# Output stores on SyncE's queue and a new order of the steps in a gated-linear-attention and hard-swish kernel

## Chip, cores and metric

The kernel runs on one core of a Trainium2 chip. The metric is the device time of one execution in microseconds; three executions of the kernel before took 554.13, 555.63 and 557.94 us. The profile shown is of one further execution, whose span is 554.3 us and which took 556.35 us by the timing. The clock granted to TensorE was 0.999 of full speed throughout.

## What is computed

A recurrent attention with decay over 4 batches, 8 heads, 768 tokens and head dimension 48, whose result is fed as 3072 tokens of 384 features to a two-layer block with a hard-swish gate. Cut to what matters:

```python
for t in range(S):
    state = alpha[:, :, t, :, None] * state + np.einsum('bhd,bhe->bhde', k[:, :, t], v[:, :, t])
    y[:, :, t] = np.einsum('bhd,bhde->bhe', q[:, :, t], state)
...
x = np.ascontiguousarray(attn_out.transpose(0, 2, 1, 3)).reshape(B * S, H * D)
h = x @ w_in                      # 384 -> 2048
relu6 = np.clip(h + 3.0, 0.0, 6.0)
g = h * relu6 / 6.0
return (g @ w_out).astype(np.float32)   # 2048 -> 384
```

All is in float32.

## The kernel before

**Chunks and groups.** The 3072 tokens are cut into 24 chunks of 128 (six to a batch), and two chunks make one of 12 groups of 256 tokens. The attention goes chunk by chunk. The two-layer block goes group by group. The first group and the preparation of the weights are the opening; this text says "behind the opening" for what comes from the step P.1.0 on.

**The attention of one chunk j.** Loads bring alpha, k and q (`la`, `lk`, `lq`: four DMAs each from chunk 6 on, line 284) and v (`lv`: eight DMAs from chunk 8 on, line 299). VectorE (DVE) transposes them in blocks of 32 (`tk`, `tq`, `ca`, line 318), runs two scans over alpha (`r` line 341, `p` line 352) and scales k and q with them (`k`, `q`, line 364). TensorE (PE) forms the scores (`sc`, lines 383 and 385), DVE masks them (`m`, line 391), and PE multiplies them with v (`yi`, lines 529 and 533; `yx` adds the part of the earlier state, line 549). For the state, k is turned by DVE (`kt`), written to DRAM and read back in another layout (`kw` line 459, one DMA; `kr` line 466, four DMAs), PE multiplies it with v (`u`, line 488), DVE adds (`sm`, line 509), GpSimd (POOL) applies the decay (`st`, line 471). `vh` (line 399) copies half of v on ScalarE (ACT), and `cy` (line 557) copies the chunk's output out of PSUM.

The products of `sc`, `yi`, `yx` and `u` use parts of the 128 x 128 array (tiles of 48 x 64, 128 x 32 and less). They are many and short: 32 matmuls for a `sc` or a `u`, 64 for a `yi`, 24 for a `yx`. This text calls them small-tile products, and a stretch of such steps on PE with no full-array product between them a run.

**The two-layer block of one group g.** The first layer is done with 20 products instead of 24 block products (`M.g.i.bank`, line 693; four column blocks and two matmul records each, eight records to a step), on sums of the inputs (`xc`) and of the weights (`y`). ACT copies some products to SBUF (`n`, line 699), DVE joins them (`o`, lines 630 to 634), ACT and DVE apply the gate (`e` line 587, `h` line 591). The second layer has seven products instead of eight (`P.g.i`, line 796, sixteen records to a step) on sums of the gated values (`s`, lines 740 and 757). `K` (line 775, ACT) saves parts, `G` (line 812 on DVE, and 809 on ACT for G.g.3) adds them up into one of four buffers `oh`, and `O` (`store2`, line 817) stores that quarter of the group's output. Stores of the opening's group are `so` (`store`, line 620).

**What sets the order.** The program is a list of words, each a step with its numbers, written out by hand under a manual schedule. Each step issues its instructions to its engines in the order of the list; every engine goes through its own instructions strictly in that order, and waits where a tile isn't ready or a buffer not yet free. A last number in a word chooses a buffer: one of four PSUM banks for full products (`M`, `P`), one of four for the small ones (`sc`, `u`, `yi`), a slot in SBUF or an `oh` buffer. Loads go through SyncE's queue (SP). In the kernel before, the stores go through ACT's queue, in between ACT's copies and gates.

```python
    def store2(g, i):
        row, col = PLACES[i]
        j = G * g + row
        nc.scalar.dma_start(out=out[j * C : (j + 1) * C, col * HD : (col + 1) * HD],
                            in_=oh_t.pop((g, i)))
```

Of the kernel before, what the change touches and what calls it, by code (L numbers as in the profile page):

```python
# [8 lines left out]
FP = mybir.dt.float32  # L9
# [8 lines left out]
def kernel(  # L18
# [32 lines left out]
    nc = tc.nc  # L51
    B, H, S, D = q.shape
    NTOK, DM = out.shape
    C = 128
# [6 lines left out]
    G = 2  # L61
# [7 lines left out]
    consts = ctx.enter_context(tc.tile_pool(name="consts", bufs=1))  # L69
# [15 lines left out]
    v0 = consts.tile([C, H, 64], FP, tag="vfirst")  # L85
# [42 lines left out]
    st, sm = [], []  # L128
# [490 lines left out]
    def store(c):  # L619
        nc.scalar.dma_start(out=out[c * C : (c + 1) * C, :], in_=os_t.pop(c))  # L620
# [193 lines left out]
    def store2(g, i):  # L814
        row, col = PLACES[i]
        j = G * g + row
        nc.scalar.dma_start(out=out[j * C : (j + 1) * C, col * HD : (col + 1) * HD],
                            in_=oh_t.pop((g, i)))
# [22 lines left out]
    with tc.manual_schedule():  # L841
# [20 lines left out]
               so.1 b.0.2 lv.7.0 y.4 y.13 ca.6 yx.5 y.0 b.0.3 cy.5 r.6 la.8 bo.0 cy.4 x.1 y.3 lv.8.1  # L862
               P.1.0.3 s.1.0.0 s.1.1.1 P.1.3.0 xc.2.1 x.2 K.1.0 s.1.2.3 xc.2.3 tk.7 s.1.3.2 P.1.2
               K.1.1 y.10 y.8 P.1.1.2 y.9 y.16 xc.2.4 s.1.4 P.1.4 x.3 K.1.2 y.15 s.1.5 xc.2.5 P.1.5
               G.1.1.0 P.1.6 G.1.3.1 y.17 y.19 G.1.0.2 y.18 y.12 y.20 M.2.0.1 tq.7 G.1.2.3 M.2.15.2
               M.2.16 lv.6.2 n.2.0.8 xc.2.6 y.21 y.23 M.2.1 xc.2.0 lk.6 lq.8 tk.6 xc.2.7 M.2.7.0 k.6
               xc.2.8 ca.7 xc.2.9 xc.2.2 r.7 vh.8 n.2.1.9 M.2.2 O.1.2 n.2.7.10 o.2.4.0 p.6 ca.8 lq.9
               la.10 la.9 lk.8 lk.9 xc.2.10 kb.6.0 M.2.8 O.1.1 n.2.2.11 M.2.3 M.2.4 n.2.4.12 o.2.0.0
               k.7 y.14 q.6 e.2.0.0 h.2.0 M.2.18.3 M.2.17 M.2.5 n.2.5.13 ck.6 M.2.9 o.2.1.0 e.2.1.1
               kb.7.3 sc.6.2.1 M.2.10 ck.7 u.6.0 u.7.3 n.2.10.14 M.2.11 n.2.11.15 p.7 m.6 q.7  # L870
               sc.7.1.2 M.2.12 n.2.18.12 M.2.19 y.22 M.2.6.1 h.2.1 n.2.12.11 M.2.13 sm.6 r.8 y.24
               o.2.3.0 m.7 tq.8 yi.6.0 yi.7.1 n.2.13.11 cy.6 st.7 yx.7 o.2.7.0 o.2.2.0 o.2.5.0 cy.7
               xc.3.0 xc.3.1 o.2.2.1 e.2.2.0 xc.3.3 o.2.7.1 M.2.14 xc.3.4 xc.3.5 o.2.3.1 P.2.0.3
               M.3.0.2 xc.3.10 xc.3.6 xc.3.7 M.3.7.1 n.3.0.11 M.3.1 o.2.6.0 h.2.2 o.2.6.1 e.2.3.1
               h.2.3 e.2.4.0 h.2.4 tk.8 xc.3.2 e.2.5.1 e.2.7.0 h.2.7 xc.3.8 n.3.1.12 n.3.7.9 K.2.0
               P.2.1.0 h.2.5 G.2.0.3 e.2.6.0 h.2.6 M.3.2 n.3.2.13 s.2.1.10 s.2.0.14 sm.7 s.2.3.15
               M.3.8 k.8 M.3.3 M.3.4 n.3.4.8 P.2.3.0 o.3.0.0 xc.3.9 p.8 s.2.2.10 M.3.9 o.3.1.0
               e.3.1.1 M.3.5 P.2.2 M.3.10 tq.9 kt.8 kw.8 lq.10 lv.9.2 n.3.5.14 K.2.2 s.2.5 P.2.5
               s.2.4 q.8 ca.9 r.9 e.3.0.0 h.3.0 p.9 O.1.0 n.3.10.10 M.3.11 K.2.1 G.2.2.0 P.2.4 tk.9
               q.9 k.9 h.3.1 n.3.11.15 M.3.12 ca.10 n.3.12.8 o.3.3.0 M.3.6.2 M.3.18.0 n.3.18.13  # L880
               sc.8.2.0 sc.9.1.3 M.3.13 M.3.19 n.3.13.8 kr.8 la.12 kt.9 kw.9 m.8 m.9 st.8 u.8.0 sm.8
               st.9 o.3.3.1 o.3.5.0 yi.8.2 yx.8 vh.9 yi.9.1 e.3.5.0 o.3.2.0 tq.10 o.3.6.0 o.3.2.1
               G.2.1.2 cy.8 yx.9 cy.9 M.3.15.0 o.3.7.0 M.3.16 M.3.14 P.2.6 o.3.4.0 M.3.17 xc.4.1
               xc.4.0 xc.4.3 e.3.3.1 o.3.6.1 h.3.3 e.3.2.1 O.2.2 O.2.1 G.2.3.0 xc.4.4 xc.4.5 xc.4.6
               xc.4.7 M.4.0.2 P.3.0.1 M.4.7.3 h.3.2 o.3.7.1 xc.4.8 h.3.5 n.4.0.8 M.4.1 e.3.6.1
               P.3.1.0 lk.10 lv.11.1 lk.11 lq.11 tk.10 e.3.7.0 h.3.7 O.2.0 e.3.4.0 n.4.7.13 xc.4.10
               r.10 p.10 k.10 s.3.1.10 h.3.4 q.10 h.3.6 tq.11 K.3.0 G.3.0.2 n.4.1.14 M.4.2 kr.9
               u.9.3 lv.10.0 s.3.0.12 kt.10 sm.9 xc.4.2 s.3.3.11 xc.4.9 s.3.2.15 st.10 sc.10.0.2
               m.10 n.4.2.9 M.4.3 M.4.4 P.3.3.0 K.3.2 M.4.8 n.4.4.10 P.3.2 K.3.1 O.3.0 so.0 s.3.4
               o.4.0.0 s.3.5 la.11 ca.11 r.11 M.4.9 o.4.1.0 e.4.1.0 tk.11 ca.12 k.11 M.4.5 P.3.5  # L890
               M.4.10 n.4.10.12 e.4.0.1 kw.10 lv.12.2 lk.12 kr.10 lk.13 lq.12 la.13 p.11 q.11
               G.3.2.3 r.12 h.4.1 P.3.4 G.3.1.2 M.4.11 M.4.18.0 vh.10 yi.10.1 tk.12 p.12 yx.10
               u.10.3 sc.11.0.2 k.12 kt.12 lq.13 lv.14.0 kw.12 tq.12 h.4.0 m.11 O.3.1 n.4.11.11
               M.4.12 n.4.12.15 P.3.6 G.3.3.2 M.4.13 n.4.5.9 n.4.18.10 O.1.3 q.12 sm.10 o.4.3.0
               o.4.7.0 M.4.6.1 o.4.3.1 n.4.13.15 vh.11 o.4.2.0 o.4.2.1 e.4.3.0 M.4.15.2 M.4.16
               M.4.19 cy.10 yi.11.0 st.11 yx.11 sc.12.2.3 o.4.4.0 h.4.3 e.4.2.1 h.4.2 O.2.3 cy.11
               xc.5.1 o.4.5.0 o.4.6.0 M.4.14 xc.5.3 xc.5.4 xc.5.5 xc.5.0 o.4.6.1 e.4.6.0 vh.12
               P.4.0.1 K.4.0 M.5.0.0 M.4.17 xc.5.7 tk.13 M.5.7.3 xc.5.6 h.4.6 m.12 e.4.5.1 n.5.0.15
               M.5.1 n.5.1.9 o.4.7.1 ca.13 h.4.5 r.13 e.4.7.0 n.5.7.14 h.4.7 e.4.4.1 O.3.2 P.4.1.2
               h.4.4 s.4.0.10 G.4.0.1 M.5.2 la.14 kr.12 u.12.1 yi.12.0 n.5.2.8 M.5.3 M.5.4 n.5.4.12  # L900
               ca.14 xc.5.8 p.13 M.5.8 s.4.1.11 P.4.3.2 o.5.0.0 xc.5.2 M.5.9 k.13 s.4.2.13 kt.13
               xc.5.10 s.4.3.10 P.4.2 K.4.1 K.4.2 e.5.0.0 O.4.0 tq.13 o.5.1.0 M.5.10 xc.5.9 M.5.5
               s.4.5 P.4.5 q.13 n.5.10.11 M.5.11 r.14 lq.14 lv.13.1 e.5.1.1 cy.12 n.5.11.10 n.5.5.13
               lk.14 tk.14 s.4.4 h.5.0 p.14 sm.12 tq.14 P.4.4 h.5.1 q.14 k.14 st.13 vh.13 M.5.12
               n.5.12.12 M.5.6.0 sc.13.2.3 m.13 sc.14.0.1 o.5.3.0 M.5.13 G.4.1.0 o.5.3.1 G.4.2.3
               n.5.13.8 o.5.2.0 o.5.2.1 yi.13.2 yx.13 cy.13 xc.6.1 xc.6.3 kw.13 lk.15 kr.13 la.15
               u.13.3 M.5.18.2 M.5.14 P.4.6 lv.15.2 la.16 sm.13 st.14 lq.16 ca.15 n.5.18.12 o.5.6.0
               xc.6.4 o.5.6.1 e.5.6.0 xc.6.5 kt.14 xc.6.0 xc.6.6 o.5.7.0 G.4.3.1 M.5.19 M.6.0.0
               xc.6.7 h.5.6 xc.6.8 o.5.5.0 tk.15 M.5.15.3 M.5.16 xc.6.2 lq.15 tq.15 o.5.4.0 n.6.0.8
               vh.14 M.6.1 e.5.2.1 n.6.1.12 P.5.0.1 h.5.2 m.14 r.15 k.15 e.5.3.0 M.6.2 e.5.4.1 h.5.4  # L910
               O.3.3 M.6.7.2 M.5.17 o.5.7.1 p.15 h.5.3 n.6.2.15 M.6.3 n.6.7.9 M.6.8 q.15 e.5.5.1
               h.5.5 K.5.0 M.6.4 n.6.4.14 O.4.3 o.6.0.0 e.5.7.0 kw.14 ca.16 P.5.1.3 M.6.9 M.6.5
               sc.15.2.3 yi.14.0 yx.14 kr.14 u.14.1 s.5.0.13 kt.15 G.5.0.2 h.5.7 o.6.1.0 e.6.1.1
               s.5.1.11 s.5.2.10 P.5.3.3 sm.14 xc.6.10 M.6.10 lk.16 lv.17.1 xc.6.9 tk.16 s.5.4
               s.5.3.13 P.5.2 s.5.5 O.5.0 n.6.10.11 M.6.11 K.5.2 O.4.2 h.6.1 r.16 n.6.5.15 e.6.0.0
               kw.15 kr.15 lk.17 la.18 k.16 p.16 m.15 M.6.18.0 n.6.18.10 o.6.6.0 tk.17 tq.16 h.6.0
               n.6.11.13 o.6.7.0 q.16 K.5.1 P.5.5 kt.16 G.5.2.1 M.6.12 P.5.4 n.6.12.14 M.6.19
               o.6.5.0 o.6.3.0 M.6.13 n.6.13.10 st.15 la.17 ca.17 M.6.6.3 o.6.2.0 r.17 sc.16.1.2
               vh.15 yi.15.3 cy.14 yx.15 lq.17 lv.16.0 kw.16 u.15.0 lk.18 lv.19.2 lk.19 sm.15 st.16
               o.6.3.1 G.5.1.2 cy.15 xc.7.1 xc.7.3 M.6.15.0 M.6.14 xc.7.4 o.6.6.1 M.6.16 o.6.4.0  # L920
               e.6.4.1 e.6.3.0 o.6.2.1 xc.7.5 xc.7.6 P.5.6 M.6.17 xc.7.10 h.6.4 M.7.0.2 e.6.2.1
               n.7.0.14 h.6.2 h.6.3 xc.7.0 xc.7.8 m.16 e.6.6.1 xc.7.9 o.6.7.1 xc.7.7 e.6.5.0 G.5.3.3
               O.5.2 h.6.6 h.6.5 s.6.0.10 s.6.2.9 P.6.0.3 M.7.1 n.7.1.12 P.6.1.1 M.7.2 e.6.7.1 h.6.7
               k.17 s.6.1.15 P.6.3.0 K.6.0 G.6.0.1 s.6.3.8 n.7.2.11 M.7.7.1 K.6.2 M.7.3 M.7.4
               n.7.7.13 O.5.1 M.7.8 P.6.2 O.4.1 O.6.0 n.7.4.10 tq.17 p.17 s.6.5 tk.18 o.7.0.0 ca.18
               xc.7.2 e.7.0.0 M.7.9 M.7.5 n.7.5.15 s.6.4 q.17 sc.17.3.0 kr.16 lq.18 o.7.1.0 M.7.10
               K.6.1 n.7.10.8 vh.16 e.7.1.1 P.6.4 M.7.11 u.16.1 n.7.11.9 yi.16.2 vh.17 yx.16 cy.16
# [84 lines left out]
```

## Time and profile before

| | before |
|---|---|
| median of three runs | 555.63 us |
| span of the profiled execution | 554.3 us |
| PE, matmul records busy | 539.9 us (97%) |
| PE, weight loads busy | 512.7 us (93%) |
| DVE busy | 474.6 us (86%) |
| ACT busy | 205.0 us (37%) |
| POOL busy | 56.1 us (10%) |
| DMA moved | 52.82 MB, mean 95 GB/s |

How to read it: a row of a timeline gives the start of a stretch of equal instructions and how long the stretch is; matmuls are pipelined, so one record (326 ns in line 796) overlaps the next, and the pace is seen from the distance between starts. In a row of waits the number ahead of the last comma counts the waits and the last is the longest. "issue" as the releaser means that the engine waited for nothing that the profile shows. PEld is the weight load, a second instruction for each matmul. SPq and ACTq are the sequencers' own rows, which issue DMAs. A chain of waits follows the last instruction back, step by step, to what released it.

### The profile page before, as it was taken

Reading aid. Unit: us, or ns where it says so; the run is one execution under the profiler, and the core shown is the slowest. Engines: PE = TensorE matmul, PEld = TensorE weight load, DVE = VectorE, ACT = ScalarE, POOL = GpSimd, SP = SyncE. Lnnn points to the kernel's source line nnn. Section 1 sums busy time; section 2 is a strip of 40 time slices with the busy share of each in tenths; the row PEclk is TensorE's granted clock in tenths of the full one; section 3 lists DMA queues with packets and bytes.
Section 4 is the critical chain, followed back from the end, with each engine's and each line's share of the span. In section 5 each row is a group of like instructions: output and inputs, shape, how many; then the busy total and the mean of one; then the engine's idle time right before and its main releaser. Section 6 shows DMA issues by size and latency. Waiting matters only on the chain.

```text
span 554.3 us, 14864 instructions
## 1 busy us (share of the span) xinstructions
PE 539.9 (97%) x6222; PEld 512.7 (93%) x6222; DVE 474.6 (86%) x822; ACT 205.0 (37%) x358; POOL 56.1 (10%) x76
## 2 busy tenths in 40 slices
PE   8989999999999999999999999999999999999997
PEld 8789886699999899899999999999899899999997
DVE  6978997999999999899999998897899678756381
ACT  2487672104342332252251343333324333233230
POOL 3334346000100000000100000000100100000000
PEclk9999999999999999999999999999999999999999
DMA  8998678232303355343444434053234310000001
GB/s 176 200 200 172 197 240 211 57 73 67 81 0 80 96 127 136 97 119 94 99 117 109 101 84 110 26 136 99 62 86 116 88 33 8 8 31 2 10 19 44
DMA packets 98515, 52.82 MB, mean 95 GB/s; under 512 B 51472, under 2 KB 91664, under 8 KB 98448
## 3 DMA queue, kind: packets, MB, share of 16 engines
q1 hardware_dynamic: 90704, 45.18, 34.5%
q10 hardware_dynamic: 7744, 6.69, 4.1%
q8 instruction: 49, 0.80, 0.6%
q14 instruction: 18, 0.15, 0.1%
HBM read 43.71 MB, written 8.13 MB: 94 GB/s over the span
## 4 chain that ended last, share of the span: by engine, by line
PE 84%; DVE 6%; DMA 5%; issue 2%; ACT 1%; SPq 1%; ACTq 0%; POOL 0%; DVEq 0%; POOLq 0%
PE m_ps L796 32%; PE m_ps L693 29%; PE m_ps L571 6%; PE m_ps L609 4%; PE t_ps L549 2%; DMA v<-in_v_dram 2%; DMA out_dram<-oh 2%; PE m_ps L582 1%; PE t_ps L383 1%; DVE g_sb L630 1%; PE t_ps L408 1%; PE t_ps L529 1%; PE t_ps L314 1%; PE t_ps L533 1%; PE m_ps L625 1%
## 5 line engine op out<-in xcount | busy, mean ns | idle before, releaser
L796 PE MATMUL m_ps<-w,g_sb 128*128 128x192 f32 x704 | 121.5, 326 | 0.0
L796 PEld LDWEIGHTS m_ps<-w,g_sb 128*128 128x128 f32 x704 | 113.8, 190 | 0.4
L699 ACT COPY g_sb<-m_ps 128x512 f32<-128x512 f32 x110 | 63.9, 584 | 130.5 <-PE m_ps L693 108.6
L796 PE MATMUL m_ps<-rings,g_sb 128*128 128x192 f32 x528 | 91.4, 326 | 0.0
L693 PE MATMUL m_ps<-xc,w 128*128 128x128 f32 x640 | 83.7, 278 | 2.0 <-DVE oh L812 1.2
L796 PEld LDWEIGHTS m_ps<-rings,g_sb 128*128 128x128 f32 x528 | 85.3, 190 | 0.2
L587 ACT ACTIVATE r<-g_sb,half 128x512 f32<-128x512 f32 x80 | 56.7, 722 | 73.2 <-DVE g_sb L634 41.9
L693 PEld LDWEIGHTS m_ps<-xc,w 128*128 128x128 f32 x640 | 78.0, 192 | 4.3 <-DVE oh L812 1.4
L591 DVE SCALAR_TENSOR_TENSOR g_sb<-r,g_sb 128x512 f32<-128x512 f32 x80 | 53.7, 681 | 5.5 <-ACT r L587 4.4
L471 POOL TENSOR_TENSOR t<-t,R 128x384 f32<-128x384 f32 x20 | 21.8, 1088 | 360.4 <-DVE t L509 153.7
L693 PE MATMUL m_ps<-xT,raw 128*128 128x128 f32 x400 | 51.6, 276 | 0.7 <-DVE g_sb L632 0.7
L693 PEld LDWEIGHTS m_ps<-xT,raw 128*128 128x128 f32 x400 | 48.3, 192 | 1.4 <-DVE g_sb L632 1.0
L740 DVE TENSOR_TENSOR g_sb<-g_sb 128x512 f32<-128x512 f32 (+1 forms) x55 | 42.7, 802 | 2.5 <-PE m_ps L796 2.3
L693 PE MATMUL m_ps<-xT,w 128*128 128x128 f32 x320 | 42.3, 276 | 0.0
L693 PEld LDWEIGHTS m_ps<-xT,w 128*128 128x128 f32 x320 | 39.5, 192 | 0.2
L630 DVE TENSOR_TENSOR g_sb<-g_sb 128x512 f32<-128x512 f32 x40 | 27.8, 700 | 7.4 <-ACT g_sb L699 7.4
L341 DVE TENSOR_TENSOR_SCAN R<-t,ones 128x516 f32<-128x516 f32 x24 | 30.0, 1249 | 3.4 <-ACT t L332 2.0
L571 PE MATMUL m_ps<-xT,w 128*128 128x256 f32 x144 | 32.3, 381 | 0.0
L693 PE MATMUL m_ps<-xc,raw 128*128 128x128 f32 x240 | 32.1, 277 | 0.0
L352 DVE TENSOR_TENSOR_SCAN P<-t 128x516 f32<-128x516 f32 x24 | 30.3, 1262 | 0.1
L571 PEld LDWEIGHTS m_ps<-xT,w 128*128 128x128 f32 x144 | 26.9, 190 | 3.7 <-issue 0.2
L693 PEld LDWEIGHTS m_ps<-xc,raw 128*128 128x128 f32 x240 | 29.6, 192 | 0.5 <-issue 0.2
(121 smaller groups left out, 740.3 us busy)
## 6 DMA issues: line engine op xcount, KB each, us to landing
raw<-in_moe_w_out_dram SPq DMA_DIRECT2D x8, 768.0 KB, 4.4
out_dram<-oh ACTq DMA_DIRECT2D x44, 96.0 KB, 2.1
raw<-in_moe_w_in_dram SPq DMA_DIRECT2D x18, 192.0 KB, 4.2
qq<-in_q_dram SPq DMA_DIRECT2D x36, 96.0 KB, 2.6
aq<-in_alpha_dram SPq DMA_DIRECT2D x36, 96.0 KB, 2.6
kq<-in_k_dram SPq DMA_DIRECT2D x36, 96.0 KB, 2.5
far<-kq SPq DMA_DIRECT2D x13, 256.0 KB, 2.1
kb<-far SPq DMA_DIRECT2D x52, 64.0 KB, 2.2
```

What stands on the lines that cost most here:

```text
L341: nc.vector.tensor_tensor_scan(out=reverse(R, n - 1, n), data0=reverse(ax, n, n), data1=reverse(ones, n, n), initial=0.0, op0=ALU.mult, op ...
L352: nc.vector.tensor_tensor_scan(out=P_t[j], data0=aX[j % 2][:, 0:n], data1=ini[j % 2], initial=0.0, op0=ALU.mult, op1=ALU.add)
L471: nc.gpsimd.tensor_tensor(out=st[j % 2], in0=sm[j % 2], in1=R_t[j][:, :, 0:1].to_broadcast([C, NP, 2 * D]), op=ALU.mult)
L571: nc.tensor.matmul(h[:, f], w1[:, kk, o : o + C], xT_t[g][:, kk], start=(kk == 0), stop=(kk == KT - 1))
L587: nc.scalar.activation(out=to, in_=h, func=AF.Relu, bias=half, scale=1.0 / 6.0)
L591: nc.vector.scalar_tensor_tensor(out=to, in0=r, scalar=1.0, in1=h, op0=ALU.min, op1=ALU.mult)
L609: nc.tensor.matmul(o_t[c], gs[0][:, f, c * C : (c + 1) * C], w2[:, f], start=(f == 0), stop=(f == NF - 1))
L630: eng.tensor_tensor(out=out, in0=in0, in1=in1, op=ALU.add if s1 > 0 else ALU.subtract)
L693: nc.tensor.matmul(acc[g][i][:, f * C : (f + 1) * C], spots[w][:, f * C : (f + 1) * C], x_of(g, x), start=(first and f == 0), stop=last, s ...
L699: nc.scalar.copy(out=slots[z], in_=acc[g][i])
L740: nc.vector.tensor_tensor(out=out, in0=in0, in1=in1, op=ALU.subtract)
L796: nc.tensor.matmul(to[g], a, rhs[:, f], start=(first and f == 0), stop=(last and f == HF - 1), skip_group_check=True)
```

## The change

Two edits, and a third without any effect on the program (a name is given to a tile). The two functions that store now issue from SP's queue:

```diff
-        nc.scalar.dma_start(out=out[c * C : (c + 1) * C, :], in_=os_t.pop(c))
+        nc.sync.dma_start(out=out[c * C : (c + 1) * C, :], in_=os_t.pop(c))
...
-        nc.scalar.dma_start(out=out[j * C : (j + 1) * C, col * HD : (col + 1) * HD],
+        nc.sync.dma_start(out=out[j * C : (j + 1) * C, col * HD : (col + 1) * HD],
                             in_=oh_t.pop((g, i)))
```

And the list of words is another from behind the opening on (the first 300 of its 1665 words are the same). The same steps stand in both, with other places and other buffer numbers. Around chunks 8 and 9, and at the end:

```diff
-               sc.8.2.0 sc.9.1.3 M.3.13 M.3.19 n.3.13.8 kr.8 la.12 kt.9 kw.9 m.8 m.9 st.8 u.8.0 sm.8
-               st.9 o.3.3.1 o.3.5.0 yi.8.2 yx.8 vh.9 yi.9.1 e.3.5.0 o.3.2.0 tq.10 o.3.6.0 o.3.2.1
-               G.2.1.2 cy.8 yx.9 cy.9 M.3.15.0 o.3.7.0 M.3.16 M.3.14 P.2.6 o.3.4.0 M.3.17 xc.4.1
...
-               s.11.5 G.11.0.1 K.11.1 O.10.0 P.11.4 K.11.2 G.11.1.0 P.11.5 G.11.2.2 O.11.2 G.10.3.3
-               O.11.0 O.10.3 O.11.1 P.11.6 G.11.3.3 O.11.3""")
...
+               O.1.2 O.1.0 kw.8 lk.10 kr.8 sm.7 r.9 st.8 sc.8.2.3 m.8 s.2.4 h.3.0 K.2.1 n.3.10.8
+               M.3.11 M.3.15.1 M.3.16 n.3.11.14 yi.8.0 O.1.1 yx.8 lq.10 la.10 tq.9 lq.11 G.2.2.3
+               O.2.2 k.9 p.9 u.8.1 M.3.12 sm.8 kt.9 kw.9 q.9 h.3.1 M.3.18.0 n.3.18.15 P.2.4 G.2.1.2
+               ca.10 sc.9.2.3 m.9 M.3.19 o.3.5.0 n.3.12.9 vh.9 M.3.13 st.9 yi.9.1 yx.9 o.3.4.0
...
+               P.11.2 e.11.2.0 e.11.3.1 h.11.2 h.11.3 P.11.1.3 s.11.5 K.11.1 P.11.4 K.11.2 P.11.5
+               G.11.1.3 G.11.2.2 P.11.6 G.11.3.1 O.11.3 G.11.0.0 O.11.2 O.11.0 O.11.1""")
```

The runs of small-tile products behind the opening, old and new, by their count and length in matmuls: before 24 runs of 240, 208, 208, 176, 152, 152, 152, 120, 120, 120, 96, 96, 88, six of 64, three of 32 and two of 16; after 26 runs: seven of 152, 128, 120, 120, 96, five of 88, five of 64, 56, 32, 32, 16, 16 (a full product's step stands between any two of them). The longest before are u.20 yi.20 yx.20 u.21 yi.21 yx.21, u.8 yi.8 yx.8 yi.9 yx.9 and u.16 yi.16 yx.16 yi.17 yx.17.

## The prediction

> **What bounds the kernel now.** I read the busy shares, then the waits of TensorE (PE), then PE's timeline at its pauses, then the waits of the queue of SyncE (SP).
>
> The page's first part, the instruction queue's row of its third part, and rows of the waits (who waits, for whom, us in all, times, longest):
>
> ```profile
> PE 539.9 (97%) x6222; PEld 512.7 (93%) x6222; DVE 474.6 (86%) x822; ACT 205.0 (37%) x358; POOL 56.1 (10%) x76
> ...
> q8 instruction: 49, 0.80, 0.6%
> ...
> PE t_ps L549 <- issue: 2.5, 2, 1.3
> ...
> PE m_ps L693 <- DVE oh L812: 1.2, 1, 1.2
> PE t_ps L529 <- ACT v L399: 1.0, 1, 1.0
> PE m_ps L693 <- ACT g_sb L699: 0.8, 1, 0.8
> ```
>
> PE is the bound, and its waits are short and few. PE's timeline in three places (start us, us, instruction, count, idle before):
>
> ```profile
> 144.08 1.16 PE L693 MATMUL m_ps<-xc,w 128*128 128x128 f32 x8
> 145.07 1.06 PE L693 MATMUL m_ps<-xT,w 128*128 128x128 f32 x8
> 145.97 1.06 PE L693 MATMUL m_ps<-xc,w 128*128 128x128 f32 x8
> 146.86 1.06 PE L693 MATMUL m_ps<-xc,raw 128*128 128x128 f32 x8
> 147.85 1.95 PE L539 MATMUL t_ps<-A,v 128*32 128x128 f32 x64
> ...
> 186.49 0.83 PE L549 MATMUL t_ps<-q,t 128*32 128x128 f32 x21
> 188.50 0.41 PE L549 MATMUL t_ps<-q,t 128*32 128x128 f32 x3 [1.19 <-issue]
> ...
> 438.75 0.40 PE L549 MATMUL t_ps<-q,t 128*32 128x128 f32 x7
> 440.49 0.71 PE L549 MATMUL t_ps<-q,t 128*32 128x128 f32 x17 [1.34 <-issue]
> ```
>
> The first five give the price of a full-array step by its distance to the next start: 0.89 us among its like (145.97 to 146.86), 0.99 just behind or just ahead of small tiles. The last four show a small-tile step stopping halfway (21 of 24 done, 7 of 24 done) with nothing awaited. The same happens inside L533 at 352.7 us. These three stops lengthen their steps by 1.58, 0.84 and 1.61 us, 4.0 us together.
>
> SP's queue, as waits, and its timeline (one row is one step):
>
> ```profile
> SPq L284 <- DMA out_dram<-oh: 24.0, 8, 8.6
> SPq L284 <- DVE oh L812: 8.6, 1, 8.6
> ...
> 218.48 1.80 SPq L284 DMA_DIRECT2D kq<-in_k_dram  x4
> 220.32 7.38 SPq L284 DMA_DIRECT2D qq<-in_q_dram  x4
> 227.75 1.85 SPq L284 DMA_DIRECT2D aq<-in_alpha_dram  x4
> ...
> 223.98 0.34 ACTq L817 DMA_DIRECT2D out_dram<-oh  x1
> 224.36 0.59 ACT L699 COPY g_sb<-m_ps 128x512 f32<-128x512 f32 x1 [3.67 <-DVE oh L812]
> ```
>
> Loads wait for stores although the stores stand on ScalarE's (ACT's) queue: the trace's semaphores show eight that all DMAs of both queues take in turn, each DMA waiting for the one eight before it. So the store that left at 223.98, once its sum was ready, held the fourth q load until 227.39 (four issues in 7.38 us instead of 1.80), and ahead of it on ACT a copy stood 3.67 us behind the same store.
>
> **What the Trainium skill says.** "Runtime: NRT & Kernel Launch", Instruction fetch mechanics: instructions come in blocks of 256 (16 KiB), and the cost is mostly hidden. The trace agrees with the block (49 packets, 0.80 MB) and shows where it isn't hidden: I counted PE's instructions in program order, and the three stops are all at the same remainder of 256, each at the end of a block that lay wholly in small tiles. "TensorEngine Tiling (Array Packing)", Key Properties: a change of tiling mode drains the array; above it costs 0.10 us on either side. "DMA: Bandwidth & Descriptors", Issuing engines are not separate DMA queues: moving an issue saves only the sequencer's time, here 0.34 us on ACT. "Trainium Kernel Development and Optimization", Reading a trace, distrusts matmul busy time; so I use distances between starts, not the 97%.
>
> **The base of the sum.** Behind the opening, from P.1.0 at 108.04 us to the last step P.11.6 (starts 548.03, 2.6 us long), PE takes 442.6 us. Taking each step at its shortest distance in this trace with the same kinds of neighbours (0.89 a first product, 2.60 a second one, 0.66 a yx, 0.89 to 0.92 a yi, 0.34 to 0.47 a u, 0.67 to 0.85 a sc) gives 432.7. So 9.9 us are pauses: 4.0 in the three stops, 2.4 around 235 and 245 us (yi.11 with yx.11, M.5.1), 2.2 at 401 and 414 us (before M.8.6 and M.8.17), 1.3 in crumbs. All of it, 1.8%, is what a new order can gain at most.
>
> **Part 1: shorter runs of small tiles.** Behind the opening the old list has 24 runs of small-tile steps, the longest with 240, 208, 208, 176 and three times 152 matmuls; the new one has 26, seven of 152 and none longer. A matmul and its weight load are two instructions, so a run needs over 128 matmuls to hold a whole block. The excess over 128 is 392 matmuls before (784 instructions, 784/256 = 3.1 blocks expected, 3 seen) and 7 x 24 = 168 after (336 instructions, 1.3 blocks expected). At 1.3 us each (4.0/3) that leaves 1.7 us: gain 2.3. Bounds: none hit (gain 4.0), three hit (0); where the blocks fall depends on semaphore instructions that I can't count beforehand.
>
> **Part 2: more changes of mode.** Two more runs at about 0.3 us (0.10 on each side, 0.1 at the last small step) are 0.6; inside the runs the kind of tile changes 26 times instead of 17, at some 0.1 us (a yx ahead of a sc takes 0.85 instead of 0.66, a yx ahead of a u none more). Step by step the new list adds to 434.3 by the same prices: loss 1.6 us. Nothing hides it, for PE is the path.
>
> **Part 3: the stores on SP.** 46 issues leave ACT (0.34 us each, 15.5 us); ACT is 37% busy, so this gains nothing itself, but copies no longer queue behind a store that waits for its sum. SP gets 46 issues of about 0.4 us, 18 us beside 206 us of loads behind the opening. Where SP is densest, from M.4.0 to M.6.0, it has 70 us of issues in 82 us of PE's work before, and 80 in 85 us after, 3 to 6 us of it stores. A store there now holds all loads behind it until its sum is ready, not only from the eighth DMA on, but no longer until it has landed (1.6 to 3.9 us later). The new order puts most stores of that stage well behind their sums (by PE's work between them: O.2.0 70 us, O.3.2 37, O.3.3 36, O.4.0 30; O.2.2, O.4.2, O.4.3 and O.5.0 close behind), so SP should rarely wait. The 5.7 us in which SP stood still at 221.7 to 227.4 made q's transpose (the first DVE step behind it) 2.0 us late, and I take the 2.4 us of pauses at 235 and 245 as its echo: gain 2.4, bounds 0 and 2.4.
>
> **Part 4: the rest of the order.** VectorE's (DVE's) own work due by each PE step: the tightest after the first 10 us is P.2.1, 49.8 us of DVE for 48.6 of PE before, and P.2.3, 54.1 for 55.1, after; with DVE 2.1 us ahead at the start (105.9 against 108.0) the spare is 0.9 and 3.1 us. At M.8.6 it is 16.0 and 14.9, plus 2.1. DVE stays just off the path. Loads with less than 3 us of PE's work ahead of their first use: 17 before, 13 after. On the other side, PSUM banks are reopened sooner: openings within 2 us of PE's work after the product whose reader frees the bank are 8 before, 18 after (five of them at 0.9 us, as M.8.0 behind P.6.6). A reader takes 0.32 to 0.59 us, so each can just be in time; the crumbs seen are 0.12 to 0.15 us, so ten more cost 1.5 (bounds 0 and, if each waits for one more DVE step of 0.6 us, 6). For kr.13 and la.11 I sum SP's issues from the last thing that they wait for and get landings 0.5 us late each: about 0.6 us for both. The pauses at 401 and 414 us I leave as they are: 0, bounds minus 2.2 and plus 3.
>
> **Part 5: the end.** Chain of waits at the end, before:
>
> ```profile
> 549.54 1.70 DMA out_dram<-oh
> 551.25 0.02 issue
> 551.27 0.02 ACTq L809
> 551.28 0.04 issue
> 551.33 0.32 ACT oh L809
> ```
>
> The last copy waited about 0.5 us for the store that held its buffer; in the new list its buffer was stored a group earlier: gain 0.5. But on SP three stores (O.11.2, O.11.0, O.11.1) now stand behind O.11.3, which waits for that copy: three issues of 0.43 us later: loss 1.3. Net loss 0.8, bounds 0.3 and 1.5.
>
> **Sum.** 554.3 - 2.3 + 1.6 - 2.4 + 1.5 + 0.6 + 0.8 = 554.1 us of span, a change of -0.2. The span's own execution stands at 556.35 us in the timing, the median of the three runs is 555.63 (554.13 to 557.94); I subtract 0.2 from the median and get 555.4, rounded to 555.5.
>
> **Rivals.** *The stores block the loads (slower).* For: SP has only 5 us to spare between M.4.0 and M.6.0, and four stores there follow their sums closely. Against: SP runs some 10 us ahead of the list elsewhere. If SP falls behind by one halt of the size seen (5.7 us) in two places, DVE loses its spare of 3 us in each and PE pauses about 5 us altogether; with none of the 2.4 gained and three blocks stopping (2.3 not gained), 554.1 + 5 + 2.4 + 2.3 = 563.8 span, 565 at the median. It decides from about 6 us of new PE pauses. *All pauses go (faster).* For: loads stand earlier, ACT is free of stores, DVE has more spare early. Then 9.9 - 1.6 - 0.8 = 7.5 us are gained: 546.8 span, 548 at the median. Against: 18 tight bank openings. *The order does nothing for instruction fetch*, blocks falling badly in the new runs: 4.0 stays, 557.8 at the median, still within 1%.
>
> **How the numbers follow.** Forecast with its bad-block variant 0.57 (own range 551 to 560), stores block loads 0.23, all pauses go 0.20. A difference under 1% is about what a measurement of this kernel can't tell from no change; 1% is 5.6 us. Faster by over 1% (below 550.1) 0.2, slower (over 561.2) 0.23, within 0.57. The range that leaves out two in ten is 548.5 to 563.
>
> **What would show it.** Right: no "issue" wait over 0.5 us in L549 or L533, or one at most; distances of 0.99 us at more steps; hardly any wait of SP for out_dram landings; three issues after the last copy. Wrong: new PE waits for DVE oh or ACT g_sb above 6 us in total, long SP waits for DVE oh with DVE waiting for q, k or alpha loads behind, or PE pauses below 4 us in all.

## The result, and the profile after

| | median | ratio to before | interval (95%) |
|---|---|---|---|
| before, four runs beside it | 555.88 us | | |
| after, four runs | 549.29 us (547.93 to 551.47) | 0.9884 | 0.9836 to 0.9932 |

The changed kernel is 1.2% faster. The time lies inside the predicted range of 548.5 to 563, but only 0.8 us above its lower end and not where the forecast put it: the forecast was no change, and the rival "all pauses go" (548 us) is what happened.

The page of the changed kernel: busy shares, the row of the instruction queue, and the engines' shares in the chain that ended last.

```profile
PE 541.3 (98%) x6222; PEld 513.9 (93%) x6222; DVE 470.2 (86%) x822; ACT 203.2 (37%) x358; POOL 55.2 (10%) x76
...
q8 instruction: 49, 0.80, 0.6%
...
PE 94%; issue 2%; DMA 2%; ACT 1%; SPq 0%; ACTq 0%
```

PE is the bound even more than before, and the 49 instruction blocks are fetched as before. All waits of PE in the changed kernel (who, for whom, us, times, longest):

```profile
PE t_ps L494 <- ACT kb L437: 1.8, 1, 1.8
PE m_ps L625 <- POOL ident masks.py:199: 1.5, 1, 1.5
PE t_ps L539 <- DVE A L416: 0.2, 1, 0.2
PE t_ps L314 <- DMA rings<-in_q_dram: 0.2, 1, 0.2
```

All four lie in the opening. The two "issue" rows of L549, and those that waited for DVE and ACT in L693 and L529, have gone. The waits of SP's queue for the sums that it is to store, between 108 and 436 us, the stretch in which there are loads to be held up:

```profile
SPq L817 <- DVE oh L812: 3.0, 2, 2.1
```

Its timeline around the last loads:

```profile
430.03 1.88 SPq L284 DMA_DIRECT2D kq<-in_k_dram  x4
431.95 15.07 SPq L817 DMA_DIRECT2D out_dram<-oh  x4
```

Where loads follow, the new list lets no store wait for more than 2.1 us. From 431.95 us SP has only stores left; the second row, which the window's end cuts off, has O.6.1, O.8.1, O.8.3 and O.8.2. SP then stands in front of a store for up to 34 us, which holds nothing but other stores. The same waits over the whole execution:

```profile
SPq L817 <- DVE oh L812: 82.4, 6, 34.4
```

**The account.** From P.1.0 to the end of P.11.6, I again take each step at its shortest distance among like neighbours, now over both traces. Before: 432.0 us and 10.6 us of pauses above it. After: 433.6 and 1.1, no single pause over 0.12. So 9.5 us of pauses went and more changes of mode cost 1.6. The tail, from PE's end to the end of the execution, grew from 3.45 to 4.46 us: 1.0. These give -6.9 us, against -6.6 at the medians. The profiled execution's span fell by only 4.6, because its opening, whose words are the same but for the last five, took 2.3 us longer (see the last section).

### The profile page after: what moved, and what is told of

The parts are those of the page before. It is cut to its first block, busy times and chain, and to the rows that moved or that the text cites. A ratio compares the mean times of both kernels' runs of the same rounds, so it can differ in the third digit from the quotient of the medians.

```text
span 549.7 us, 14906 instructions
## 1 busy us (share of the span) xinstructions
PE 541.3 (98%) x6222; PEld 513.9 (93%) x6222; DVE 470.2 (86%) x822; ACT 203.2 (37%) x358; POOL 55.2 (10%) x76
## 4 chain that ended last, share of the span: by engine, by line
PE 94%; issue 2%; DMA 2%; ACT 1%; SPq 0%; ACTq 0%
PE m_ps L796 35%; PE m_ps L693 33%; PE m_ps L571 6%; PE m_ps L609 4%; PE m_ps L582 2%; PE t_ps L549 2%; PE t_ps L383 2%; PE t_ps L529 2%; PE t_ps L408 2%; PE t_ps L533 1%; DMA rings<-in_k_dram 1%; PE t_ps L314 1%; PE t_ps L539 1%; PE t_ps L488 1%; DMA rings<-in_q_dram 1%
## 5 line engine op out<-in xcount | busy, mean ns | idle before, releaser
L693 PE MATMUL m_ps<-xc,w 128*128 128x128 f32 x640 | 82.8, 277 | 0.0
L693 PEld LDWEIGHTS m_ps<-xc,w 128*128 128x128 f32 x640 | 77.9, 192 | 1.6 <-issue 1.2
L693 PE MATMUL m_ps<-xT,raw 128*128 128x128 f32 x400 | 52.3, 277 | 0.0
L693 PEld LDWEIGHTS m_ps<-xT,raw 128*128 128x128 f32 x400 | 48.7, 192 | 0.5
L693 PE MATMUL m_ps<-xT,w 128*128 128x128 f32 x320 | 42.6, 277 | 0.0
L693 PEld LDWEIGHTS m_ps<-xT,w 128*128 128x128 f32 x320 | 39.4, 192 | 0.6 <-issue 0.2
L693 PE MATMUL m_ps<-xc,raw 128*128 128x128 f32 x240 | 32.1, 277 | 0.0
L630 DVE TENSOR_TENSOR g_sb<-m_ps,g_sb 128x512 f32<-128x512 f32 x30 | 20.5, 683 | 11.3 <-ACT g_sb L699 8.8
L693 PEld LDWEIGHTS m_ps<-xc,raw 128*128 128x128 f32 x240 | 29.6, 192 | 0.4
```

The source lines that it names most:

```text
L630: eng.tensor_tensor(out=out, in0=in0, in1=in1, op=ALU.add if s1 > 0 else ALU.subtract)
L693: nc.tensor.matmul(acc[g][i][:, f * C : (f + 1) * C], spots[w][:, f * C : (f + 1) * C], x_of(g, x), start=(first and f == 0), stop=last, s ...
```

## The experiments

Stops are what PE loses with nothing awaited where a block of its instructions ends, mostly in the middle of a step. All pauses are counted behind the opening, over the same shortest distances. Each ratio is to executions of before that were timed beside that run. The excerpts of the list are cut to the words around a move.

| run | list | stores | median | ratio (95%) | pauses | of these, stops |
|---|---|---|---|---|---|---|
| before | old | ACT | 555.88 | | 10.6 | 4.0 |
| after | new | SP | 549.29 | 0.9884 (0.9836 to 0.9932) | 1.1 | 0 |
| e1 | new | ACT | 563.71 | 1.0148 (1.0084 to 1.0213) | 15.2 | 0 |
| e2 | old | SP | 566.69 | 1.0214 (1.0139 to 1.0289) | 22.5 | 4.0 |
| e7 | new, 5 stores later | ACT | 551.12 | 0.9927 (0.9902 to 0.9952) | 3.4 | 0 |
| e8 | old, 3 stores moved | SP | 553.50 | 0.9968 (0.9954 to 0.9982) | 8.5 | 4.0 |
| e9 | old, 2 stores moved | SP | 554.51 | 0.9982 (0.9959 to 1.0005) | 8.5 | 3.3 |
| e3 | old, runs split | ACT | 553.70 | 0.9953 (0.9930 to 0.9976) | 8.2 | 0.7 |
| e4 | old, blocks shifted | ACT | 553.19 | 0.9951 (0.9931 to 0.9971) | 7.0 | 1.2 |
| e10 | new, blocks shifted | SP | 549.17 | 0.9883 (0.9850 to 0.9915) | 3.0 | 1.8 |
| e11 | old, DVE earlier | ACT | 554.05 | 0.9966 (0.9942 to 0.9990) | 9.6 | 4.5 |
| e5 | new, tail reordered | SP | 546.18 | 0.9841 (0.9818 to 0.9864) | 1.3 | 0 |
| a1 | new, once more | SP | 548.32 | 0.9889 (0.9862 to 0.9915) | 1.1 | 0 |

### Each half alone: e1 and e2

e1 is the new list with the old queue (against after):

```diff
-        nc.sync.dma_start(out=out[j * C : (j + 1) * C, col * HD : (col + 1) * HD],
+        nc.scalar.dma_start(out=out[j * C : (j + 1) * C, col * HD : (col + 1) * HD],
```

e2 is the old list with the new queue (against before; in both the other store function goes likewise):

```diff
-        nc.scalar.dma_start(out=out[j * C : (j + 1) * C, col * HD : (col + 1) * HD],
+        nc.sync.dma_start(out=out[j * C : (j + 1) * C, col * HD : (col + 1) * HD],
```

> The new list, with the two store functions back on ScalarE's (ACT's) queue. PE's program is then that of the changed kernel. Theory (the order does it: shorter runs take the three stops for instruction fetch away, 4.0 us, and stores placed well behind their sums, earlier loads and more spare take the other pauses, 5.5 us; the queue is worth little): no stop inside a small-tile step, PE pauses behind the opening under 2.5 us, median 549 to 551 us, with the tail about 0.8 us shorter than in the changed kernel since the last store no longer has three others queued behind it in the same way. Rival (the queue is worth the 2.4 us of pauses at 235 and 245 us, because on ACT's queue a store holds ACT's copies and, from eight DMAs on, the loads): pauses of 2 to 4 us come back around the stores of M.4 and M.5, median 551.5 to 553.

> The old list, with only the stores moved to SyncE's (SP's) queue. Theory: the three stops inside small-tile steps stay at 186, 352 and 438 us (4.0 us), and so do the pauses that come from the order; what can go is at most the 2.4 us at 235 and 245 us: median 553 to 555.6. Rival A (the queue, not the order, removed everything but the stops): PE pauses 4.0 us or little more, median 549.5 to 550.5. Rival B (with stores close behind their sums, as the old list has them, a store at the head of SP's queue holds the loads behind it until its sum is ready): new PE or DVE waits for q, k or alpha loads, median above 557.

Both halves alone make the kernel slower, by 7.8 and 10.8 us; together they gain 6.6. None of the expectations foresaw this for e1. For e2, rival B has the median (above 557), but only a part of the cause. e1's ACT, timeline:

```profile
427.74 0.32 ACT L775 COPY u<-m_ps 128x192 f32<-128x192 f32 x1 [0.61 <-PE m_ps L796]
427.75 11.65 ACTq L817 DMA_DIRECT2D out_dram<-oh  x4
439.44 0.59 ACT L699 COPY g_sb<-m_ps 128x512 f32<-128x512 f32 x1 [11.38 <-DVE oh L812]
```

and e1's PE:

```profile
440.08 2.08 PE L693 MATMUL m_ps<-xc,w 128*128 128x128 f32 x8 [5.43 <-ACT g_sb L699]
441.95 4.25 PE L796 MATMUL m_ps<-w,g_sb 128*128 128x192 f32 x16
```

The last two of these four stores, O.6.1 and O.8.1, are the first two of the row at 431.95 on SP, where O.8.1 waited as well. On ACT's queue they stand ahead of the copy `n.9.11`. O.8.1 waits for its sum on DVE; ACT stands idle for 11.38 us ahead of the copy, and PE has no free bank: 5.6 us, and 2.5 more in the next steps, which run slower than their kind. The same happens at 491 (3.2 us) and 531 (0.8). In this last stage the new list puts stores directly behind their sums, which only a queue with nothing due behind them can bear.

e2's SP, two places:

```profile
182.30 5.64 SPq L817 DMA_DIRECT2D out_dram<-oh  x2
187.98 2.12 SPq L284 DMA_DIRECT2D kq<-in_k_dram  x3
...
231.41 5.32 SPq L299 DMA_DIRECT2D v<-in_v_dram  x8
236.83 0.54 SPq L459 DMA_DIRECT2D far<-kq  x1
237.41 1.92 SPq L817 DMA_DIRECT2D out_dram<-oh  x4
```

and what PE and ACT waited for:

```profile
204.36 0.58 PE L488 MATMUL t_ps<-v,kb 128*32 128x48 f32 x32 [2.42 <-DMA kb<-far]
...
239.86 2.08 PE L693 MATMUL m_ps<-xc,w 128*128 128x128 f32 x8 [7.33 <-ACT oh L809]
```

```profile
239.49 0.32 ACT L809 COPY oh<-m_ps 128x192 f32<-128x192 f32 x1 [9.83 <-DMA out_dram<-oh]
```

At 182.30 it is rival B's wait, though the load that PE misses in the end is `kb` and not q, k or alpha: two stores, in the old list ahead of lk.10, lv.11, lk.11 and lq.11, hold these loads until 187.98, and the `kb` load behind them reaches u.9 2.4 us late (4.0 us of pauses to 208, 1.5 of them in steps that run slower than their kind). At 237.41 it is the reverse: loads hold the stores. O.3.1 comes behind eight v loads and a write of `kq`; until it has landed its buffer isn't free, ACT stands idle for 9.83 us ahead of the copy `G.3.3`, ACT's other copies stand behind it, and PE has no bank (10.2 us of pauses to 246).

### Are those places all of it? e7, e8 and e9

e7, against e1; O.9.1, O.9.2, O.9.0 and O.10.1 are moved likewise:

```diff
-G.8.1.1 O.8.1 n.9.11.8
+G.8.1.1 n.9.11.8
-n.9.13.11 o.9.2.0
+n.9.13.11 O.8.1 o.9.2.0
```

e9, against e2:

```diff
-e.3.2.1 O.2.2 O.2.1 G.2.3.0
+e.3.2.1 O.2.2 G.2.3.0
-lk.11 lq.11 tk.10
+lk.11 lq.11 O.2.1 tk.10
-u.10.3 sc.11.0.2 k.12 kt.12 lq.13
+u.10.3 O.3.1 sc.11.0.2 k.12 kt.12 lq.13
-m.11 O.3.1 n.4.11.11
+m.11 n.4.11.11
```

e8 differs from e9 in that O.2.2 moves too, behind G.2.3, which uses its buffer: that quarter of the output is then G.2.3's sum.

> The new list with the stores on ScalarE's (ACT's) queue, as in e1, and five of the 46 stores put a few steps later: O.8.1 from ahead of n.9.11 to behind n.9.13, O.9.1, O.9.2 and O.9.0 from ahead of e.10.5 to behind n.10.13, O.10.1 from ahead of n.11.12 to behind n.11.13. In e1 PE lost 12.1 us at just these places (8.1 at 440 to 446, 3.2 at 491, 0.8 at 531). Theory (ACT stands at a store whose sum is late, its copies stand behind it, and PE has no free bank): these 12 us go, 1.5 to 2 us of other pauses stay, median 550 to 552. Rival (the queue itself costs, through ACT's issue time and the loads that wait for landings): less than half of it goes, median above 557.

> The old list with the stores on SyncE's (SP's) queue, as in e2, and three stores put elsewhere: O.2.2 and O.2.1 behind the loads lk.10, lv.11, lk.11 and lq.11 instead of ahead of them, O.3.1 ahead of lq.13, lv.14 and kw.12 instead of behind them. In e2 PE lost 4.0 us at 204 to 208, behind a load of kb that came late, and 10.2 us at 240 to 246, behind the copy of G.3.3 that waited 9.83 us for O.3.1's buffer. Theory (the first two stores hold loads until their sums are ready; the third is held by loads, and its buffer holds ACT and PE): both places fall below 1.5 us, the three stops for instruction fetch stay (about 4 us), median 553 to 556. Rival (SP has no room for the stores in this stage, wherever they stand): the lost time turns up at the neighbouring steps, median above 560.

> As e8, but O.2.2 stays where the old list has it, so that every store finds its own sum; only O.2.1 (behind lq.11) and O.3.1 (ahead of lq.13) are moved. Theory (in e2 it was O.2.1 at the head of SP's queue that held the loads at 182 to 188 us, and O.3.1 behind the loads that held ACT): both places stay below 1.5 us, the three stops stay at about 4 us, median 553 to 554.5, as in e8. Rival (O.2.2 mattered as well, or e8 gained by the wait that it left out): 2 to 4 us come back at 204 to 208, median above 556.

e7's ACT at the place where e1 stood for 11.65 us, and e9's SP and ACT at e2's two places:

```profile
427.32 1.40 ACTq L817 DMA_DIRECT2D out_dram<-oh  x3
429.09 0.59 ACT L699 COPY g_sb<-m_ps 128x512 f32<-128x512 f32 x1 [1.47 <-PE m_ps L693]
```

```profile
183.16 0.43 SPq L817 DMA_DIRECT2D out_dram<-oh  x1
183.63 3.23 SPq L284 DMA_DIRECT2D kq<-in_k_dram  x4
```

```profile
228.53 0.32 ACT L809 COPY oh<-m_ps 128x192 f32<-128x192 f32 x1 [2.02 <-PE m_ps L796]
```

With five of 46 stores elsewhere e1's loss of 12.1 us is gone, and with two e2's loss of 14.2. So neither queue is bad in itself; a store costs by what is queued behind it while it waits, or ahead of it while its buffer is wanted. e7 is 4.6 us faster than before, so the new list earns most of the gain on ACT's queue too. What SP is worth beyond that is the difference between e7 and a1, 2.8 us, whose intervals overlap a little: e7 keeps 2.3 us more pauses, among them two waits for `kb` loads (1.2 us), on a queue whose loads wait 12 times, 18.5 us together, for stores on ACT to land. In e9 the queue alone, with good places, gains nothing that can be measured (0.9982, interval to 1.0005): the pause at 235 us is gone and 0.6 of the 1.0 us at 242 stays, but a new wait of 1.0 us comes at P.4.4.

### The stops: e3, e4 and e10

e3, against before, one of three such moves:

```diff
-yi.8.2 yx.8 vh.9 yi.9.1
+yi.8.2 yx.8 M.3.15.0 vh.9 yi.9.1
```

e4, against before, 5 of the 24 idle products left out:

```diff
-la.0 z.3.5 lv.0.0
+la.0 lv.0.0
```

e10, against after, 8 of the 14 left out:

```diff
-tq.0.2 z.0.8 la.2
+tq.0.2 la.2
```

> The kernel before, stores on ACT, with one full-array step moved into each of its three longest runs of small-tile products: M.3.15 between yx.8 and yi.9, M.7.12 between yx.16 and yi.17, M.9.12 between yx.20 and u.21. Nothing else is changed; the work is the same. Theory (PE stops where a block of 256 instructions passes faster than the next is fetched, so the length of the run decides): the three stops of 1.58, 0.84 and 1.61 us vanish, three more changes of mode cost 0.3 us each, median about 3.1 us lower, 552.0 to 553.0. Rival (the stops come from something that these chunks wait for, such as the decayed state from GpSimd or a PSUM bank, and which the profile doesn't name): they stay in yx.9, yi.17 and yx.21, and the median is 555.6 to 557.

> The kernel before with 24 of the 29 idle products of the opening left out (they compute nothing that is used; they only keep TensorE busy in the first 20 us). Order, runs and stores are those of before. 24 idle products are 96 PE instructions, so every later block of 256 instructions ends 96 instructions further on in the list. By the durations of before, no block then lies in small tiles so that it passes in under about 3 us together with the 64 instructions ahead of it. Theory (the blocks' position decides the stops): none of the three stops, though all the long runs are still there; PE pauses behind the opening 4 us fewer, about 6 us; median 4 us lower from this, about 551.6, and up to 2.6 us lower still or, if TensorE's clock rises later in the opening without this work, up to 3 us higher. Rival 1 (the long runs stop by themselves, or wait for an engine): the stops stay in yx.9, yi.17 and yx.21. Rival 2 (the block is another size or counts otherwise): stops at other places.

> The changed kernel with 14 of the 29 idle products of the opening left out (they compute nothing that is used). That is 56 PE instructions, so that every block of 256 ends 56 instructions further on in the list. By the durations of the changed kernel's own trace three blocks then lie wholly in runs of small tiles and pass in 2.0 to 2.3 us: they end in sc.15 (near 293 us), u.20 (near 416) and u.22 (near 433). Theory A (a run of 152 matmuls can stop as well as a longer one; the changed kernel has no stop only because its blocks fall well): one to three stops at just these places, 0.3 to 1.6 us each, PE pauses of 2 to 5 us instead of 1.1, median 550 to 552. Theory B (runs up to 152 are too short to stop): none, median 548 to 549.5.

In e3 two stops went and one of 0.7 us was left, just ahead of yx.21:

```profile
434.80 1.16 PE L693 MATMUL m_ps<-xc,w 128*128 128x128 f32 x8
435.88 0.54 PE L488 MATMUL t_ps<-v,kb 128*32 128x48 f32 x32
...
436.69 0.63 PE L533 MATMUL t_ps<-A,v 128*32 128x64 f32 x32
437.84 0.86 PE L549 MATMUL t_ps<-q,t 128*32 128x128 f32 x24 [0.52 <-issue]
```

Its run (u.21 yi.21 yx.21) has only 120 matmuls, and the block that ends there has the moved M.9.12 in it. So splitting a run doesn't rule a stop out, and a stop doesn't need a block of small tiles alone. The moved M.3.15 brought a new wait of 0.8 us for its bank. In e4, whose order is untouched, the three stops vanished from their places, which no cause in chunks 9, 17 and 21 themselves would do. But "none" was wrong: PE stopped in a new place, yi.9, after 5 of the 32 products of line 529,

```profile
186.27 0.28 PE L529 MATMUL t_ps<-A,v 128*32 128x64 f32 x5
187.32 0.58 PE L529 MATMUL t_ps<-A,v 128*32 128x64 f32 x26 [0.76 <-issue]
```

and by 0.2 us in u.21, both where a block ended that lay in small tiles. Both medians fell by less than forecast (553.7 against 552 to 553 in e3, 553.2 against about 551.6 in e4). e10 is the sharper test, since it foretells places in the changed kernel, whose longest run is 152:

```profile
429.54 0.43 PE L488 MATMUL t_ps<-v,kb 128*32 128x48 f32 x23
430.54 0.30 PE L488 MATMUL t_ps<-v,kb 128*16 128x48 f32 x9 [0.56 <-issue]
```

u.22 stopped after 23 of 32 products (0.8 us) and sc.15 at 290 (0.6), two of the three places named; a block that ended inside M.5.15 cost 0.4 more. So theory A: a run of 152 can stop, and the changed kernel has no stop partly because its blocks fall well. Its median shows no clear loss (549.17 against 548.32 for a1, intervals overlapping) and lies where theory B put it; the pauses and their places carry the verdict.

### The pauses at 401 and 414 us: e11

Against before:

```diff
-e.8.0.0 h.8.0 st.19 tk.21
+e.8.0.0 h.8.0 st.19 G.7.2.0 G.7.1.3 tk.21
-h.8.1 G.7.2.0 G.7.1.3 n.8.11.10
+h.8.1 n.8.11.10
-o.8.7.0 p.21 k.21 P.8.0.0 q.21 o.8.4.0 M.8.17
+o.8.7.0 o.8.4.0 p.21 k.21 P.8.0.0 q.21 M.8.17
```

> The kernel before (old list, stores on ACT) with two places of VectorE's (DVE's) work put earlier: the sums G.7.2 and G.7.1, which free the PSUM bank of M.8.6, ahead of the decay steps tk.21, ca.21, r.21 and kt.20 instead of behind them, and o.8.4, which must read the bank before M.8.17 adds to it, ahead of p.21, k.21 and q.21. Nothing else is changed. Theory (these two DVE orders made the pauses at 401 and 414 us, 1.35 and 0.83 us in the kernel before): both pauses go, the three stops and those at 235 and 245 us stay, PE pauses 2 us fewer, median 553 to 554.5. Rival (DVE is late there as a whole, so what is put ahead only delays the rest): the pauses move to M.8 to M.9's other steps or to chunk 21's yi, median unchanged within 0.5 us.

M.8.6 and M.8.17 in before, then M.8.18 and M.8.17 (with M.9.2) in e11:

```profile
401.08 1.16 PE L693 MATMUL m_ps<-xc,w 128*128 128x128 f32 x8 [1.19 <-DVE oh L812]
414.36 1.83 PE L693 MATMUL m_ps<-xT,raw 128*128 128x128 f32 x14 [0.66 <-DVE g_sb L632]
```

```profile
401.13 1.16 PE L693 MATMUL m_ps<-xc,w 128*128 128x128 f32 x8 [0.51 <-ACT g_sb L699]
412.10 1.95 PE L693 MATMUL m_ps<-xT,raw 128*128 128x128 f32 x16
```

Both pauses (1.35 and 0.83 us in the trace of before) are gone from M.8.6 and M.8.17; 0.7 and 0.2 us turn up at M.8.18 and M.9.0. So they came from the place of three DVE steps behind a chunk's transposes and scans, and this part of the old list was worth some 1.3 us. The median fell by 2.1 us, more than the pauses explain; the rest isn't accounted for.

### The tail: e5 and a1

e5, against after; a1 is the changed kernel unaltered:

```diff
-P.11.6 G.11.3.1 O.11.3 G.11.0.0 O.11.2 O.11.0 O.11.1
+P.11.6 G.11.0.0 O.11.2 O.11.0 O.11.1 G.11.3.1 O.11.3
```

> The changed kernel with its last eight words in another order: G.11.0, O.11.2, O.11.0 and O.11.1 ahead of G.11.3 and O.11.3, so that the store that waits for the last copy is the last issue on SP's queue and not the fourth from the last. Theory: the last landing comes three issues of about 0.43 us earlier, 1.0 to 1.3 us in the tail from the last matmul to the end (4.46 us there, 3.45 in the kernel before). Rival (the landing of the last store, not the issues behind it, sets the end): no gain, within 0.3 us.

> The changed kernel once more, beside e5 and e7. Its opening took 2.3 us longer than that of before in the first profile, with the same words. Expected of theory: that difference is scatter of one execution, so P.1.0 begins between 106 and 110 us; PE pauses behind the opening about 1 us again, no stop inside a small-tile step; median 549 to 550.

The last issues of SP in the changed kernel and in e5, whose last copies end at 545.62 and 541.54 us:

```profile
520.37 27.06 SPq L817 DMA_DIRECT2D out_dram<-oh  x7
```

```profile
538.96 2.94 SPq L817 DMA_DIRECT2D out_dram<-oh  x4
```

The last issue ends 1.81 us behind the copy in the one and 0.36 in the other. The tail is 2.99 us in e5 and 4.46 in a1: 1.5 us gained, a little over the forecast. The queue has no part in it: e1, whose tail was expected to be 0.8 us shorter, has 4.4 us, with the same three stores behind O.11.3 on ACT. The medians differ by 2.1 us (546.18, 545.89 to 546.51, against 548.32, 547.65 to 551.7). e5 is the fastest version of the study.

## Why the prediction was right and wrong

The sum said -0.2 us; the medians say -6.6. By its steps:

- **Base** (9.9 us of pauses is all that order can gain): right. With the shorter distances that both traces give it is 10.6, and 9.5 of it went.
- **Part 1** (1.7 us of stops stay): 0 stayed. That the place of the blocks decides was right, and the shift of blocks in e4 and e10 shows it. The condition was too narrow: a run was said to need over 128 matmuls, and e3 stopped in one of 120. The term was an average over where blocks fall; in this list none falls badly, which is luck and not a merit of the shorter runs alone: e10, with blocks 56 instructions further on, has 1.8 us, the predicted size.
- **Part 2** (+1.6): measured +1.6.
- **Part 3** (-2.4, the echo at 235 and 245): all of it went. It did not take SP's queue, for e1 has none of it either. The fear of stores blocking loads was wrong for the new list, for the reason given: its stores stand well behind their sums. For the old list it was right in part: that e2's 566.7 us lies near the 565 that this rival gave for the new list is luck, since held loads make only 4.0 of e2's 14.2 us and a held store the rest. What the step missed is how much hangs on it. "This gains nothing itself" was wrong: with this list, ACT's queue costs 15 us (e1 against a1; 2.8 with five stores moved, e7), as on ACT a waiting store holds copies, and PE's banks with them. The place cited from the Trainium skill ("DMA: Bandwidth & Descriptors", Issuing engines are not separate DMA queues) says that moving an issue saves only the sequencer's time; here the wait at the queue's head moves with it, 11.65 us in e1.
- **Part 4** is the step that failed. It charged 1.5 us for ten more tight bank openings and 0.6 for kr.13 and la.11, and left 2.2 us at 401 and 414 as they are and 1.3 in crumbs. Measured: no pause over 0.12 us, so the charges were 0 and the 2.2 went. A reader of 0.32 to 0.59 us does come just in time for a bank reopened 0.89 us later, when its engine isn't late. And I left the two pauses because I didn't ask what they wait for: e11 shows that the place of three DVE steps decides, which could be read from both lists beforehand (the old list has o.8.4 directly ahead of M.8.17, the new one three products ahead).
- **Part 5** (+0.8): +1.0 in the trace, and e5 shows the cause, three issues behind the last copy.

Parts 1 and 4 together are 1.7 + 1.5 + 0.6 + 2.2 = 6.0 of the 6.7 us between the forecast and the account of -6.9. All these errors lie on one side: where a step could cost or not, I charged it.

## What to carry to other kernels

A DMA issue that must wait is priced by what stands behind it on its queue and by who wants its buffer, so a change of queue and the list of steps must be judged together: each half of this change alone cost 8 to 11 us, and both gained 7. For each pause in the old trace look up the step it waits for, and where the new order puts that step, before it is left in the sum. Put the store that depends on the last work last on its queue.

## What the runs showed of the hardware

**From the packet of a block to PE's going on it takes much the same time.** In seven stops of before, e3, e4 and e10, PE went on 2.2 to 2.7 us after the packet of the next block started (before: packet 185.96, PE 188.50; e4: 185.11 and 187.32; e10: 427.83 and 430.54), and in the twelve of e2, e8, e9 and e11 after 2.2 to 2.9. By the count of PE's instructions, a block that lies in small tiles passes in some 1.9 to 2.5 us in these traces. Whether PE stops depends on when the packet starts: 1.3 us behind the block's first instruction ahead of the stop at 187 in before, but about 0.8 us ahead of it in the changed kernel at 272, where a block of 2.2 us passed without a stop. In e3 the block took 3.1 us, but its packet came 1.5 us behind its first instruction, and PE stopped. The Trainium skill's "mostly hidden" ("Runtime: NRT & Kernel Launch", Instruction fetch mechanics) holds for the other blocks of the trace. What sets the packet's start wasn't tried.

**After a pause PE can run slower.** e2's steps behind its pause of 7.3 us (the next row is two steps):

```profile
241.73 3.62 PE L693 MATMUL m_ps<-xT,raw 128*128 128x128 f32 x16
```

A first product took 1.87, then twice 1.71 us there instead of 0.89, and e1's P.8.5 behind the pause of 5.4 us took 4.09 instead of 2.60. A pause of only 2.4 us in e2, at 204, was followed by the same (M.4.3 took 1.81), while behind e1's pause of 3.0 us, at 490, nothing of the kind is seen. The granted clock goes with it. Rows of windows have start and end, length, then busy us and counts of PE, PEld, DVE, ACT and POOL, granted clock, DMA share, GB/s; two of e2 and two of e1:

```profile
206.00:208.00 2.00, 2.00 (x21) 1.84 (x16) 2.00 (x4) 0.00 (x0) 0.82 (x1) 0.50 0.15 25
247.00:250.00 3.00, 3.00 (x101) 2.70 (x90) 1.56 (x4) 0.48 (x1) 0.00 (x0) 1.00 0.02 5
...
442.00:444.00 2.00, 2.00 (x8) 2.00 (x8) 0.00 (x0) 1.78 (x5) 0.00 (x0) 0.50 0.00 0
490.00:492.00 2.00, 1.31 (x11) 1.32 (x12) 1.81 (x3) 0.75 (x3) 0.00 (x0) 1.00 0.12 38
```

So the three pauses with a lowered clock cost 1.5 to 2.9 us more than their length. The length alone doesn't decide whether the clock falls; what does wasn't tried.

**The opening varies.** With the same words P.1.0 began between 106.1 us (e5, e7) and 110.5 us (a1, past the 106 to 110 expected). Both profiled executions of the changed kernel had the late one, with a wait of 1.8 and 2.2 us in u.1.3. Three windows of the first of them:

```profile
20.00:40.00 20.00, 18.13 (x228) 16.32 (x232) 15.28 (x26) 11.42 (x14) 6.34 (x5) 0.83 0.91 190
...
24.00:25.00 1.00, 0.62 (x17) 0.57 (x18) 0.97 (x3) 0.70 (x2) 1.00 (x1) 1.00 1.27 193
26.00:28.00 2.00, 2.00 (x17) 1.78 (x16) 1.02 (x3) 0.00 (x0) 1.11 (x2) 0.50 1.02 186
```

From 20 to 40 us the clock was 0.83 in both and 1.00 in all other traces. The wait came first: it ended at 24.38 us, and the clock was 1.00 until 25 us and 0.50 from 26 us on. Whether the wait made it fall wasn't tried. The two executions are the slowest of their kernel in the timings (551.47 and 551.70 us), so the medians hardly show it.
